# First batch of an attention, FFT and MoE kernel: the local value left in PSUM, and four unfolded feature chunks

## The chip, the cores and the metric

The kernel runs on one core of one Trainium2 chip. The metric is the device time of one execution in microseconds (us), here as the median of three. The engines are TensorE (PE, matrix products), VectorE (DVE), ScalarE (ACT), GpSimd (POOL) and SyncE (SP, which issues transfers). PE adds products in PSUM; the other data lie in SBUF.

## What is computed

The program chains three blocks, over a batch of 4 with 576 tokens, 8 heads of 64 and so 512 features:

```python
def _attn_ref(q, k, v):
    q_d, k_d, v_d = means of 4 neighbouring tokens of q, k, v
    out_up = np.repeat(sm_attn(q_d, k_d, v_d), 4, axis=2)        # coarse attention
    mask = np.abs(pos[:, None] - pos[None, :]) < 4
    out_local = softmax(where(mask, scale * q @ k.T, -1e9)) @ v  # local attention
    return out_up + out_local

def _moe_ref(x, w_ch1, w_ch2):
    u = x + np.real(np.fft.fft(np.fft.fft(x, axis=1), axis=2))
    un = (u - mean(u)) / np.sqrt(var(u) + 1e-6)
    return u + np.maximum(un @ w_ch1, 0.0) @ w_ch2               # 512 -> 2048 -> 512

def _moe2_ref(x, w_val, conv_w, w_out):
    gate = sigmoid(causal convolution of x, 5 taps for each feature)
    return (gate * (x @ w_val)) @ w_out
```

(The first lines of each are put in words.) The two blocks behind the attention work on its output with heads joined: x has 576 tokens and 512 features for each of the four batches.

## The kernel before

Features lie on the 128 partitions in four chunks of 128 (two heads each); tokens run along the free axis. The work behind the attention is cut into 12 units of 192 tokens, three for each batch. The weights come as words of 64-bit numbers: DVE unpacks them (`to_f32`, `word_op`, three steps for each block of 1024 columns, tiles `W`), they are split into a high and a low 16-bit half, and products are made as high times high, high times low and low times high. The first unit is done in 32 bits instead (`ph` L1140, `pc` L1151), because its split weights aren't ready.

The first batch is written out by hand in `chain0`. Its steps have short names, and `CHAIN0` lists them in the order in which they are recorded. `ORDER` gives, for each engine, the order of all instructions of the program; `SLOT` says which buffer of a ring each tile takes. Both are tables from a planner. So an engine does its own instructions strictly in the row given and waits on others by semaphore.

The steps of the first batch that matter here. For the local part, tokens are in three groups `GROUPS = ((0,), (1, 2), (3, 4))` of windows (232, 464 and 456 tokens), with score `S`, maximum `M`, exponential `X`, normalisation `N` (DVE, `dP`), turn `T` (PE transposes into `dPT`, ACT copies to `PT`) and value `V` (PE, into `dO`). For the coarse part there are four pairs of heads, with `s`, `m`, `x`, `n` (`E` times the reciprocal sum `lsu`, on POOL, in two halves), `t` (PE `eT`, ACT copy `ET`) and `v` (PE `po`, ACT copy to `base`, one column for four tokens).

`value` puts `dO` in two PSUM tiles, `c0` and `c1`, and ACT copies them into `X` (L1481). `base` then adds the coarse output on DVE, in place, each coarse column to its four tokens (`B` steps, four for each group, L424). The Fourier transform over features and tokens goes by symmetry. `fold` adds and subtracts chunks `c` and `c + 2` into `fs` (L1582), `fold2` adds and subtracts the two ends of the sequence into `fF` (L1589). ACT takes the high half `FH` of it (L1593), DVE the low half `FL`, and `piece` multiplies them with the features of the transform `feat` into three tiles of 96 or 97 rows (`ab`, `ab`, `eT`; L1607). There are four pieces, one for each sign `sd` and chunk `c`, of 3 tiles, 2 ends and 3 products, 72 matmuls of 127 to 129 columns.

`mirrored` (L1616, L1617) makes the mirrored chunks (`mir`) in 32 bits with two matrices, `mirror` and `corner`. From the pieces come `AH` and `AL`, sums over the sequence `pp` and `pq` (L1644), `DS`, the additions `X<-X,DS` and `X<-mir,DS`, the mean `st`, and `u` (L1690), the centred input of the first unit. A record of the profile counts a 32-bit matmul twice.

Of the kernel before, what the change touches and what calls it, by code (L numbers as in the profile page):

```python
# [1909 lines left out]
```

## Time and profile before

| | us |
|---|---|
| median of three runs (673.1 to 674.92) | 673.43 |
| the profiled execution | 673.44 |
| its span in the profile | 671.6 |
| PE busy | 649.7 (97%) |
| DVE busy | 459.2 (68%) |
| ACT busy | 321.3 (48%) |
| POOL busy | 126.6 (19%) |

The profile is of one execution. Span is the time from its first to its last recorded instruction, and an engine's busy time is a share of it. Since PE is busy for nearly all of the span, the stages in which it is not, and those in which its granted clock is low, are the ones to look at. The granted clock over the span is 0.981 of full speed in the mean.

### The profile page before, as it was taken

Reading aid. Unit: us, or ns where it says so; the run is one execution under the profiler, and the core shown is the slowest. Engines: PE = TensorE matmul, PEld = TensorE weight load, DVE = VectorE, ACT = ScalarE, POOL = GpSimd, SP = SyncE. Lnnn points to the kernel's source line nnn. Section 1 sums busy time; section 2 is a strip of 40 time slices with the busy share of each in tenths; the row PEclk is TensorE's granted clock in tenths of the full one; section 3 lists DMA queues with packets and bytes.
Section 4 is the critical chain, followed back from the end, with each engine's and each line's share of the span. In section 5 each row is a group of like instructions: output and inputs, shape, how many; then the busy total and the mean of one; then the engine's idle time right before and its main releaser. Section 6 shows DMA issues by size and latency. Waiting matters only on the chain.

```text
span 671.6 us, 18209 instructions
## 1 busy us (share of the span) xinstructions
PE 649.7 (97%) x7778; PEld 580.4 (86%) x7779; DVE 459.2 (68%) x962; ACT 321.3 (48%) x985; POOL 126.6 (19%) x178
## 2 busy tenths in 40 slices
PE   7888998999999899999999999999999999999997
PEld 3566897999998787989988889998999989999895
DVE  4989999899989877657787556676347444543354
ACT  3945546695344756775244576642232212311232
POOL 0130352023221713412010263030011010000000
PEclk9958999999999999999999999999999999999999
DMA  9992352221242012404220110000210000000001
GB/s 320 394 315 118 118 202 86 103 96 67 102 123 95 11 49 66 129 1 136 86 76 2 42 47 17 3 1 2 87 53 17 2 17 18 17 2 1 18 17 48
DMA packets 23299, 52.08 MB, mean 78 GB/s; under 512 B 1855, under 2 KB 11071, under 8 KB 22194
## 3 DMA queue, kind: packets, MB, share of 16 engines
q1 hardware_dynamic: 23218, 50.91, 22.2%
q8 instruction: 61, 1.00, 0.6%
q14 instruction: 20, 0.16, 0.1%
HBM read 44.41 MB, written 8.26 MB: 78 GB/s over the span
## 4 chain that ended last, share of the span: by engine, by line
PE 78%; DVE 10%; POOL 2%; ACT 1%; issue 0%; ACTq 0%; POOLq 0%; DVEq 0%
PE ph L1176 25%; PE pc L1196 24%; PE out L1304 7%; PE val L1288 7%; DVE W L418 3%; PE pc L1151 2%; PE ab L976 2%; PE po L908 1%; PE st L1060 1%; PE dO L785 1%; PE sc L863 1%; PE pp L999 1%; PE pq L999 1%; PE eT L898 1%; PE dPT L768 1%; POOL r L421 1%
## 5 line engine op out<-in xcount | busy, mean ns | idle before, releaser
L1176 PE MATMUL ph<-uh,W 128*128 128x192 f16 x1408 | 198.0, 246 | 0.3 <-ACT uh L1104 0.3
L1176 PEld LDWEIGHTS <-W 128*128 128x128 f16 x2112 | 176.1, 98 | 8.7 <-issue 3.8
L1176 PE MATMUL ph<-ul,W 128*128 128x192 f16 x704 | 171.5, 246 | 0.9 <-DVE ul L1105 0.9
L1196 PE MATMUL pc<-hh,W 128*128 128x192 f16 x1232 | 170.1, 246 | 0.0
L1196 PEld LDWEIGHTS <-W 128*128 128x128 f16 x1848 | 154.2, 98 | 3.9 <-issue 1.7
L1196 PE MATMUL pc<-hl,W 128*128 128x192 f16 x616 | 134.0, 246 | 0.5 <-DVE hl L418 0.5
L418 DVE SCALAR_TENSOR_TENSOR hl<-ph,hh 128x384 f16<-128x384 f32 x88 | 47.6, 550 | 89.4 <-ACT hh L1180 89.2
L1180 ACT ACTIVATE hh<-ph 128x384 f16<-128x384 f32 x88 | 42.6, 490 | 117.5 <-PE ph L1176 108.0
L418 DVE SCALAR_TENSOR_TENSOR W<-X,cw,W 128x192 f32<-128x192 f32 x160 | 63.7, 438 | 9.8 <-ACT W L1251 9.3
L1288 PE MATMUL val<-yy,W 128*128 128x192 f16 x576 | 58.9, 246 | 0.7 <-DVE yy L418 0.7
L1288 PEld LDWEIGHTS <-W 128*128 128x128 f16 x576 | 48.4, 98 | 2.1 <-issue 1.1
L1304 PE MATMUL out<-W,gh 128*128 128x512 f16 x144 | 45.9, 379 | 0.0
L749 ACT ACTIVATE dP<-dS,dmx 128x64 f32<-128x64 f32 x120 | 36.4, 334 | 1.6 <-PE dPT L768 1.4
L421 POOL TENSOR_TENSOR E<-E,lsu 72x288 f32<-72x288 f32 x16 | 18.1, 1144 | 67.2 <-DVE lsu L1515 34.0
L418 DVE SCALAR_TENSOR_TENSOR W<-W,W 128x1024 int32<-128x1024 int32 x24 | 29.5, 1240 | 0.0
L1304 PE MATMUL out<-W,gl 128*128 128x512 f16 x72 | 27.3, 379 | 1.2 <-DVE gl L418 1.2
L424 POOL TENSOR_TENSOR sq<-sq 128x384 f32<-128x384 f32 (+1 forms) x12 | 10.8, 900 | 88.8 <-ACT sq L1071 88.4
L749 ACT ACTIVATION_READ_ACCUMULATOR dP<-dS,dmx 128x1 f32 x120 | 27.1, 228 | 0.0
L1151 PE MATMUL pc<-h,W 128*128 128x192 f32 x128 | 24.2, 331 | 2.6 <-DVE W L418 2.6
L1196 PE MATMUL pc<-hh,Wz 128*128 128x192 f16 x176 | 25.6, 246 | 0.0
L1304 PEld LDWEIGHTS <-gh 128*128 128x128 f16 x144 | 14.0, 98 | 12.6 <-issue 0.2
L1140 PE MATMUL ph<-u,W 128*128 128x192 f32 x128 | 23.0, 329 | 1.0 <-DVE u L1690 1.0
(286 smaller groups left out, 1196.7 us busy)
## 6 DMA issues: line engine op xcount, KB each, us to landing
W<-in_moe_w_ch_dram SPq DMA_DIRECT2D x12, 1024.0 KB
out_dram<-osb SPq DMA_DIRECT2D x17, 256.0 KB
vw<-in_vw_dram SPq DMA_DIRECT2D x8, 512.0 KB
v<-in_vp_dram SPq DMA_DIRECT2D x24, 144.0 KB
X<-in_q_dram SPq DMA_DIRECT2D x6, 576.0 KB
kT<-in_k_dram SPq DMA_DIRECT2D x4, 582.0 KB
X<-in_moe_w_ch_dram SPq DMA_DIRECT2D x2, 1024.0 KB
raw<-in_moe_w_ch_dram SPq DMA_DIRECT2D x4, 512.0 KB
```

The costliest lines, as they stand in the source:

```text
L418: return eng.scalar_tensor_tensor(out=out, in0=in0, scalar=scalar, in1=in1, op0=op0, op1=op1)
L421: return eng.tensor_tensor(out=out, in0=a, in1=b, op=ALU.mult)
L749: A.activation(out=s_[:, z, a], in_=pss[par][:, z, a], func=AF.Exp, scale=SCALE, bias=mx[:, par, z, a:a + 1], accum_out=su[:, par, z, a:a ...
L976: T.matmul(out=ps[0:n, c0:c1], lhsT=d[x][:, c, sd, e, n0:n0 + n], rhs=feat[:, w, c, c0:c1], start=(t == 0), stop=(t == 5),)
L999: T.matmul(out=ps, lhsT=d[x][0:n, i, col:col + m], rhs=seq[0:n, j, i, w, :], start=(t == 0), stop=(t == 8),)
L1140: T.matmul(out=ps[:, e], lhsT=W[AT[kc * 2 + m // 8] + 1][:, o:o + 128], rhs=u()[:, kc, :], start=(kc == 0), stop=(kc == 3))
L1151: T.matmul(out=c["ps"][m // 2][:, m % 2], lhsT=W[9 + g][:, o:o + 128], rhs=hs[g // 2][:, g % 2, e, :], start=(kk == 0 and m % 2 == 0), sto ...
L1176: T.matmul(out=ps[:, e], lhsT=w1_ap(pw, kc, 2 * g + e), rhs=uh[px][:, kc, :], start=(t == 0), stop=(t == 11))
L1180: A.activation(out=h_, in_=ps, func=AF.Relu)
L1196: T.matmul(out=ps[m // 2][:, m % 2], lhsT=w2_ap(pw, kk, m), rhs=x[px][:, e, :], start=(kk == 0 and (pw, px) == (0, 0) and m % 2 == 0), sto ...
L1288: T.matmul(out=ps[:, e], lhsT=wv_ap(pw, kc, 2 * mh + e), rhs=m_["y"][px][:, kc, :], start=(t == 0), stop=(t == 11))
L1304: T.matmul(out=ps, lhsT=(gh, gl)[px][:, kc, t * 128:(t + 1) * 128], rhs=wo_ap(pw, kc), start=(n == 0), stop=(n == 11))
```

## The change

`value` leaves `dO` in its two PSUM tiles. `value_add` adds it to the coarse output and writes `X`, six DVE operations in all, one for each group and PSUM tile; the ACT copies and the twelve `base` additions go. `fold` takes the sum and difference of the two ends straight from `X`, for each of the four feature chunks, so `fs` and its slots go. `negated` lets ACT write part of `feat` with the opposite sign. `piece` runs over four chunks: for the first two one matmul covers both signs (255 or 257 columns); for the others there are two, of 127 to 129 columns each, the second against the negated features. That makes 36 + 72 matmuls in place of 72. `CHAIN0` takes the new steps in another order, and all tables of `ORDER` are new.

```diff
@@ SLOT @@
-    "prp.E": "01201201201201202102120120120120120120121021201201201220210210210210210210210120102102102100201201201201201201201210210210",
+    "prp.E": "0120120101202102120120120120120120121021201201201220210210210210210210210120102102102100201201201201201201201210210210",
+    "accp.acc": "0012012012012012",
...
@@ CHAIN0 @@
-m2 t0 w31 w50 x2 N2 n2 v0 w22 V0 t1 T11 w12 s3 m3 T10 v1 w32 x3 t2 w51 w70 n3 V1
-w60 v2 T21 w71 T20 t3 v3 V2 w52 w61 B00 B01 C B11 w62 E B10 B21 Z B20 A fF11 fF01 gF11
-fF00 gF01 gF00 fF10 hF11 lF11 R1 hF01 hF00 lF01 gF10 lF00 R0 hF10 eF11 lF10 eF01 w72 eF00 eF10 H0 H1 L0 L1
-H2 L2 w41 I Q0 w42 Y0 U00 U01 b0 Q1 J1 a0 o0 Y1 a2 U10 J0 U11 a1 o2 a3 b2 o1
-o3 O b1 b3
+m2 t0 w31 w50 x2 N2 n2 v0 w22 t1 w12 s3 m3 v1 w32 x3 Z t2 w51 w70 n3 w60 v2 w71
+t3 v3 V0 B00 B01 T10 T11 V1 B10 B11 T20 T21 V2 B20 B21 E A - f0 h0 f2 l0 e0 h2
+f1 l2 e2 h1 f3 l1 e1 h3 l3 R0 e3 R1 w52 w61 C w62 w72 H0 H1 L0 L1 H2 L2 w41
+I Q0 w42 Y0 U00 U01 b0 Q1 J1 a0 o0 Y1 a2 U10 J0 U11 a1 o2 a3 b2 o1 o3 O b1
+b3
...
@@ def value(g) @@
-            pos = [ps_c.tile([P, 2, nt], F32, tag=f"c{x}", name="dO") for x in range(2)]
+            pos = S_["pos", g] = [ps_c.tile([P, 2, nt], F32, tag=f"c{x}", name="dO") for x in range(2)]
...
-            xx = X.rearrange("p (a x) t -> p x a t", x=2)
-            for x in range(2):
-                A.activation(out=xx[:, x, :, PAD + q0:PAD + q0 + nt], in_=pos[x], func=AF.Copy)
+
+        def value_add(g, x):
+            q0 = 2 * GROUPS[g][0] * WQ
+            n = sum(NQ[2 * p + hf] for p in GROUPS[g] for hf in range(2)) // 4
+            o = X.rearrange("p (a x) t -> p x a t", x=2)[:, x, :, PAD + q0:PAD + q0 + 4 * n]
+            v = d["base"].rearrange("p (a x) q -> p x a q", x=2)[:, x, :, q0 // 4:q0 // 4 + n]
+            add(V, o.rearrange("p a (q r) -> p a q r", r=4), S_["pos", g][x].rearrange("p a (q r) -> p a q r", r=4),
+                v.unsqueeze(3).to_broadcast([P, 2, n, 4]))
...
-        def base(g, cs):
-            q0 = 2 * GROUPS[g][0] * WQ // 4
-            n = sum(NQ[2 * p + hf] for p in GROUPS[g] for hf in range(2)) // 4
-            for c in cs:
-                x = X[:, c, PAD + 4 * q0:PAD + 4 * (q0 + n)].rearrange("p (g r) -> p g r", r=4)
-                add(V, x, x, d["base"][:, c, q0:q0 + n].unsqueeze(2).to_broadcast([P, n, 4]))
...
-        def fold(sd, c):
-            s_ = F["s", sd, c] = prp.tile([P, S + 1], F32, tag="E", name="fs", bufs=3)
-            V.tensor_tensor(out=s_, in0=X[:, c, PAD:PAD + S + 1], in1=X[:, c + 2, PAD:PAD + S + 1],
-                            op=(ALU.add, ALU.subtract)[sd])
-
-        def fold2(sd, c):
-            s_ = F["s", sd, c]
-            F[sd, c] = mainp["tap"].tile([P, 2, HALF], F32, tag="tap", name="fF")
+        def fold(c):
+            F[c] = mainp["tap"].tile([P, 2, HALF], F32, tag="tap", name="fF")
             for e in range(2):
-                V.tensor_tensor(out=F[sd, c][:, e], in0=s_[:, 0:HALF], in1=s_[:, S:S - HALF:-1],
+                V.tensor_tensor(out=F[c][:, e], in0=X[:, c, PAD:PAD + HALF], in1=X[:, c, PAD + S:PAD + S - HALF:-1],
                                 op=(ALU.add, ALU.subtract)[e])
...
+        def negated():
+            fh["neg"] = acc_t("neg", [P, 2, 2, 256], F16)
+            for e in range(2):
+                A.activation(out=fh["neg"][:, :, :, 128 * e:128 * e + 128], in_=feat[:, :, :, FC[2 * e + 1][0]:FC[2 * e + 1][1]],
+                             func=AF.Copy, scale=-1.0)
+
+        def piece(c):
...
             for i, (n0, n) in enumerate(TT):
                 for e in range(2):
-                    c0, c1 = FC[2 * e + sd]
+                    c0, cm, c1 = FC[2 * e][0], FC[2 * e][1], FC[2 * e + 1][1]
                     for x, w in (("FH", 0), ("FH", 1), ("FL", 0)):
...
+                        ops = [(c0, c1, feat[:, w, c, c0:c1])] if c < 2 else [
+                            (c0, cm, feat[:, w, c - 2, c0:cm]), (cm, c1, fh["neg"][:, w, c - 2, 128 * e:128 * e + 128])]
+                        for k, (p0, p1, r) in enumerate(ops):
+                            T.matmul(
+                                out=fh["ab"][i][0:n, p0:p1], lhsT=d[x][:, c, e, n0:n0 + n], rhs=r,
...
```

The rows of the order below give line, operation, output, inputs and size; a line of the changed kernel is some 30 higher than the same line before. Names: `vw_156` and `vw_158` are the values of the second and third local group, `E_498` the third pair of heads, and `E_585` (before) or `E_551` (after) the fourth.

On PE, before, from the third pair's value to the mirror matmuls:

```order
L1533 MATMUL po<-ET,vr 64x144 x4
L1475 MATMUL dO<-PT,vw_156 64x58 x7
L1524 MATMUL eT<-eye,E_498 72x72 x8
L479 MATMUL tot<-ss_v_461,ones 128x1
L1475 MATMUL dO<-PT,vw_156 64x58 x25
L1533 MATMUL po<-ET,vr 64x144 x4
L1456 MATMUL dPT<-eye,dP 128x128 x8
L1475 MATMUL dO<-PT,vw_158 64x58 x24
L1475 MATMUL dO<-PT,vw_158 64x54 x8
L1524 MATMUL eT<-eye,E_585 72x72 x8
L1533 MATMUL po<-ET,vr 64x144 x4
L1616 MATMUL mir<-X,mirror 128x287
```

The same place on PE after the change:

```order
L1558 MATMUL eT<-eye,E_551 72x72 x8
L1567 MATMUL po<-ET,vr 64x144
L1485 MATMUL dPT<-eye,dP 128x128 x4
L1567 MATMUL po<-ET,vr 64x144 x3
L1504 MATMUL dO<-PT,vw_156 64x58 x2
L1485 MATMUL dPT<-eye,dP 128x128 x8
L1504 MATMUL dO<-PT,vw_156 64x58 x30
L1485 MATMUL dPT<-eye,dP 128x128 x4
L1504 MATMUL dO<-PT,vw_158 64x58 x12
L1504 MATMUL dO<-PT,vw_158 64x54 x4
L1646 MATMUL mir<-X,mirror 128x287
```

The fourth pair's turn and value moved from behind both local values to ahead of them, and the second group's turn from ahead of the third pair's value to behind the fourth's.

On DVE, before, from the last base additions to the low halves:

```order
L424 TENSOR_TENSOR X<-X,base 128x228 x2
L424 TENSOR_TENSOR X<-X,base 128x116
L424 TENSOR_TENSOR X<-X,base 128x232
L424 TENSOR_TENSOR X<-X,base 128x228 x2
L1582 TENSOR_TENSOR fs<-X 128x577 x3
L1589 TENSOR_TENSOR fF<-fs 128x289 x4
L473 TENSOR_SCALAR s_x_766<-p2b 128x1
L1589 TENSOR_TENSOR fF<-fs 128x289 x2
L1582 TENSOR_TENSOR fs<-X 128x577
L418 SCALAR_TENSOR_TENSOR FL<-fF,s_x_766,FH 128x2x289
L1589 TENSOR_TENSOR fF<-fs 128x289 x2
L418 SCALAR_TENSOR_TENSOR FL<-fF,s_x_766,FH 128x2x289 x2
```

The same place on DVE after the change:

```order
L453 TENSOR_TENSOR X<-dO,base 128x2x232 x2
L546 TENSOR_SCALAR W_117<-W_121 128x1024
L453 TENSOR_TENSOR X<-dO,base 128x2x228
L502 TENSOR_SCALAR s_x_563<-p2b 128x1
L1610 TENSOR_TENSOR fF<-X 128x289
L453 TENSOR_TENSOR X<-dO,base 128x2x228
L1610 TENSOR_TENSOR fF<-X 128x289 x3
L502 TENSOR_SCALAR iv_x_564<-p2b 128x1
L447 SCALAR_TENSOR_TENSOR FL<-fF,s_x_563,FH 128x2x289
L1610 TENSOR_TENSOR fF<-X 128x289 x4
L447 SCALAR_TENSOR_TENSOR FL<-fF,s_x_563,FH 128x2x289 x3
```

The four `fs` are gone, the additions read `dO`, and one step of unpacking stands among them.

On DVE in the later place, just ahead of the `ul` of the first unit of the second batch, before (tile names with their numbers):

```order
L796 TENSOR_REDUCE qkT_2973<-kT_2974 128x288
L418 SCALAR_TENSOR_TENSOR hl_3372<-ph_3345,hh_3370 128x384
L796 TENSOR_REDUCE qkT_2973<-X_2970 128x288
L418 SCALAR_TENSOR_TENSOR W15_121<-W17_122,s_wv_2648,W15_121 128x1024
L418 SCALAR_TENSOR_TENSOR yy_2827<-X_132,s_y0_2713,yy_2827 128x768
L418 SCALAR_TENSOR_TENSOR W15_121<-W17_122,s_wv_2648,W15_121 128x1024
L469 TENSOR_SCALAR p2a_4531<-bq1_4527 128x1
L752 TENSOR_SCALAR dsu_3039<-dsu_3039 128x8
L473 TENSOR_SCALAR iv_y0_2714<-p2b_2717 128x1
L421 TENSOR_TENSOR uc_2586<-uc_2586,r0_2600 128x768
L418 SCALAR_TENSOR_TENSOR W17_122<-W19_123,s_wo_2692,W17_122 128x1024
L1105 TENSOR_TENSOR ul_2613<-uc_2586,uh_2612 128x768
```

The same place on DVE after the change:

```order
L657 TENSOR_REDUCE cvmx_2665<-po_2656 128x1
L447 SCALAR_TENSOR_TENSOR tap_2769<-X_132,cw_108,tap_2769 128x192 x2
L447 SCALAR_TENSOR_TENSOR hl_3307<-ph_3280,hh_3305 128x384
L447 SCALAR_TENSOR_TENSOR hl_3391<-ph_3364,hh_3389 128x384
L447 SCALAR_TENSOR_TENSOR W15_121<-W17_122,s_wv_2667,W15_121 128x1024 x2
L447 SCALAR_TENSOR_TENSOR tap_2769<-X_132,cw_108,tap_2769 128x192
L447 SCALAR_TENSOR_TENSOR X_132<-pc0_2820,iv12_1525,X_132 128x2x192
L450 TENSOR_TENSOR uc_2605<-uc_2605,r0_2619 128x768
L447 SCALAR_TENSOR_TENSOR W17_122<-W19_123,s_wo_2711,W17_122 128x1024
L1134 TENSOR_TENSOR ul_2632<-uc_2605,uh_2631 128x768
```

The two reductions `qkT` and the operation on `yy` no longer stand here, and an addition to `X` does; `yy` now comes 28 rows ahead of `ul`.

## Rows read from the trace of the kernel before

**Rows 1.** Busy time by stage: start and end, length, then each engine's busy time

```profile
core 0: us, PE busy (x) PEld busy (x) DVE busy (x) ACT busy (x) POOL busy (x), PEclk, DMA share, GB/s
40.00:50.00 10.00, 9.30 (x148) 7.77 (x148) 8.60 (x18) 4.43 (x12) 2.80 (x3) 0.50 1.02 301
50.00:60.00 10.00, 8.03 (x44) 5.85 (x42) 9.28 (x22) 5.86 (x12) 0.00 (x0) 0.69 0.53 212
...
80.00:100.00 20.00, 20.00 (x215) 18.90 (x214) 19.93 (x28) 7.78 (x25) 11.76 (x14) 1.00 0.64 215
...
200.00:240.00 40.00, 36.80 (x452) 31.42 (x451) 35.99 (x62) 22.93 (x52) 16.31 (x31) 1.00 0.16 61
300.00:400.00 100.00, 99.84 (x1378) 90.84 (x1376) 69.50 (x149) 50.87 (x176) 23.01 (x31) 1.00 0.20 64
```

**Rows 2.** The same view of two single microseconds under the mirror matmuls

```profile
55.00:56.00 1.00, 1.00 (x4) 0.71 (x3) 1.00 (x4) 0.00 (x0) 0.00 (x0) 0.50 0.36 147
56.00:57.00 1.00, 1.00 (x5) 0.83 (x4) 1.00 (x5) 0.70 (x2) 0.00 (x0) 0.90 0.08 33
```

**Rows 3.** PE's waits over the span: us in total, times, longest

```profile
PE pc L1151 <- DVE W L418: 2.6, 2, 1.7
...
PE out L1304 <- DVE gl L418: 1.2, 2, 0.7
...
PE ph L1176 <- DVE ul L1105: 0.9, 1, 0.9
...
PE ab L1607 <- DVE FL L418: 0.6, 2, 0.3
```

**Rows 4.** Chain of waits of the first 125 us: start, length, what

```profile
61.49 1.12 PE ab L1607 x20
62.61 0.35 PE eT L1607 x6
...
67.43 1.14 PE pq L1644 x9
...
72.28 0.96 DVE u L1690
...
117.14 0.92 PE pc L1151 x4
```

**Rows 5.** PE's timeline: start, length, operation, records, idle time before it with its releaser

```profile
38.96 1.44 PE L1524 MATMUL eT<-eye,E 72*72 72x72 f32 x8 [1.19 <-ACT E L1509]
...
42.36 1.23 PE L1533 MATMUL po<-ET,vr 72*64 72x144 f32 x8
43.52 1.97 PE L1456 MATMUL dPT<-eye,dP 128*128 128x128 f32 x8
46.18 1.97 PE L1475 MATMUL dO<-PT,vw 64*64 64x58 f32 x64 [0.69 <-ACT PT L1459]
...
52.43 1.30 PE L1616 MATMUL mir<-X,mirror 128*128 128x287 f32 x2 [1.40 <-DVE X L424]
...
57.76 0.28 PE L1607 MATMUL ab<-feat,FH 128*96 128x128 f16 x2
```

**Rows 6.** POOL's timeline, the normalisations of the coarse part, each half one operation

```profile
20.22 2.56 POOL L421 TENSOR_TENSOR E<-E,lsu 72x288 f32<-72x288 f32 x4 [18.78 <-DVE lsu L1515]
35.77 3.75 POOL L421 TENSOR_TENSOR E<-E,lsu 72x288 f32<-72x288 f32 x2 [12.99 <-DVE lsu L1515]
41.76 2.14 POOL L421 TENSOR_TENSOR E<-E,lsu 72x288 f32<-72x288 f32 x1 [2.23 <-DVE lsu L1515]
```

**Rows 7.** DVE's timeline, first batch

```profile
51.39 1.20 DVE L424 TENSOR_TENSOR X<-X,base 128x116 f32<-128x116 f32 x4 [0.46 <-ACT base L1535]
52.51 2.09 DVE L1582 TENSOR_TENSOR fs<-X 128x577 f32<-128x577 f32 x3
54.52 1.56 DVE L1589 TENSOR_TENSOR fF<-fs 128x289 f32<-128x289 f32 x4
...
71.14 0.81 DVE L424 TENSOR_TENSOR X<-mir,DS 128x289 f32<-128x289 f32 x2
```

More of the change, by code (lines that the diff above doesn't have):

```diff
@@ L1580, in fold @@
-        def fold(sd, c):
-            s_ = F["s", sd, c] = prp.tile([P, S + 1], F32, tag="E", name="fs", bufs=3)
-            V.tensor_tensor(out=s_, in0=X[:, c, PAD:PAD + S + 1], in1=X[:, c + 2, PAD:PAD + S + 1],
-                            op=(ALU.add, ALU.subtract)[sd])
-        def fold2(sd, c):
-            s_ = F["s", sd, c]
-            F[sd, c] = mainp["tap"].tile([P, 2, HALF], F32, tag="tap", name="fF")
+            d["FH"] = mp.tile([P, 4, 2, 290], F16, tag="M", name="FH")
+            d["FL"] = mp.tile([P, 4, 2, 290], F16, tag="M", name="FL")
@@ L1595, in fold_lo, with fold_hi @@
-        def fold_lo(sd, c):
-            stt(V, d["FL"][:, c, sd, :, 0:HALF], F[sd, c], d["sx"][:, 0:1], d["FH"][:, c, sd, :, 0:HALF],
-                ALU.mult, ALU.subtract)
-        def piece(sd, c):
+        def fold_hi(c):
+            A.activation(out=d["FH"][:, c, :, 0:HALF], in_=F[c], func=AF.Copy, scale=d["sx"][:, 0:1])
+        def fold_lo(c):
+            stt(V, d["FL"][:, c, :, 0:HALF], F[c], d["sx"][:, 0:1], d["FH"][:, c, :, 0:HALF], ALU.mult, ALU.subtract)
+        def negated():
[3 more added lines that the diff above has]
+                             func=AF.Copy, scale=-1.0)
@@ L1604, in piece @@
                 for e in range(2):
-                    c0, c1 = FC[2 * e + sd]
+                    c0, cm, c1 = FC[2 * e][0], FC[2 * e][1], FC[2 * e + 1][1]
                     for x, w in (("FH", 0), ("FH", 1), ("FL", 0)):
-                        T.matmul(
-                            out=fh["ab"][i][0:n, c0:c1], lhsT=d[x][:, c, sd, e, n0:n0 + n], rhs=feat[:, w, c, c0:c1],
-                            start=(fh["e"] == 1 and (e, x, w) == (0, "FH", 0)), stop=(fh["e"] == 4 and (e, x) == (1, "FL")),
-                        )
+                        ops = [(c0, c1, feat[:, w, c, c0:c1])] if c < 2 else [
[3 more added lines that the diff above has]
+                                out=fh["ab"][i][0:n, p0:p1], lhsT=d[x][:, c, e, n0:n0 + n], rhs=r,
+                                start=(fh["e"] == 1 and (e, x, w, k) == (0, "FH", 0, 0)),
+                                stop=(fh["e"] == 4 and (e, x, k) == (1, "FL", len(ops) - 1)),
+                            )
         def mirrored(c):
@@ L1715, in chain0 @@
         for g in range(3):
-            for h in range(2):
-                tok[f"B{g}{h}"] = lambda g=g, h=h: base(g, (h, h + 2))
-        for sd in range(2):
-            for c in range(2):
-                for n, f in (("f", fold), ("g", fold2), ("h", fold_hi), ("l", fold_lo), ("e", piece)):
-                    tok[f"{n}F{sd}{c}"] = lambda sd=sd, c=c, f=f: f(sd, c)
+            for x in range(2):
+                tok[f"B{g}{x}"] = lambda g=g, x=x: value_add(g, x)
+        for c in range(4):
+            for n, f in (("f", fold), ("h", fold_hi), ("l", fold_lo), ("e", piece)):
+                tok[f"{n}{c}"] = lambda c=c, f=f: f(c)
+        tok["-"] = negated
         for c in range(2):
```

441 lines of the change are left out of this document (234 added, 207 removed), and 3 rows, old and new, of the table ORDER.

## The prediction

> **What bounds the kernel now.** I read the busy time by stage first. From 300 to 400 us PE is busy for 99.84 of 100 us at the full granted clock (1.00): there the kernel is TensorE's own work, and nothing the change touches shortens it [rows 1]. The early stages are another matter. [...] DVE works 8.60 and 9.28 us there, and 19.93 of 20 us from 80 to 100 us [rows 1]. So up to about 118 us two things race: the chain of the first batch through PE, and DVE's unpacking of the weights. PE's waits show who ends last: 2.6 us in two waits of `pc` for an unpacked `W`; at 117.14 us the chain of waits passes to PE for good [rows 3, 4]. From 200 to 240 us PE is idle for 40.00 - 36.80 = 3.2 us [rows 1], and waits for `gl` (1.2 us) and `ul` (0.9), both DVE's, are the longest of the later part [rows 3].
>
> In the first batch three places matter. The last base additions, four operations, began at 51.39 when ACT had copied `base` (0.46 us idle), took 1.20 and ended at 52.59 [rows 7]. PE waited 1.40 us for them, then did mirror and corner matmuls from 52.43 to 57.76, then the pieces [rows 5], the last of which ended at 62.61 + 0.35 = 62.96. And `u` at 72.28 starts the first unit [rows 4].
>
> **Base is finished earlier: -3.7 us.** Before, the turn and value of the last pair of heads stand behind the last local value on PE, ACT copies local values to SBUF, and DVE adds later. Now all heads go ahead of the second and third local values, and the sum is made straight from PSUM. By the order, DVE reaches the last reciprocal `lsu` with 0.8 us more work ahead of it than it had before the third one (its normalisation on POOL began at 35.77 [rows 6]), so at about 36.4. POOL normalised four halves in 2.56 us, 0.64 each, and later two in 3.75 [rows 6]; two halves so cost 1.3 to 3.75 us, and I take 2.5, the middle, since both conditions of DVE occur here: 38.9. Then the second half of `eT` (1.44 for both), its copy by ACT, the second half of `po` (1.23 for both) and the copy to `base` [rows 5], together 2.4 with the two copies at about 0.5: 41.3. Ends are 40.1 and 43.
>
> From there: the first additions 0.3 (later ones run beside PE), the eight `dPT` (1.97 in all, of which 0.5 is done by then) 1.5, the second local value like the third one now, 1.97 for 64 records and 1.85 without its last ones, four `dPT` 1.0, a copy of `PT` by ACT 0.6, and the second half of the third local value 0.95 [rows 5]: 41.3 + 0.3 + 1.5 + 1.85 + 1.0 + 0.6 + 0.95 = 47.5. The last two additions cost about 0.55 us each (456 elements; two of 289 took 0.81) with a fold of 0.39 between and the rest of the queue, 1.4 in all: 48.9 against 52.59, so -3.7 [rows 7]. Ends: -1.5 with the late base, -4.5 if PE waits for no copy.
>
> The six additions now read `dO` in PSUM, which no addition in this trace does. The nearest rows: `X<-mir,DS` (PSUM) took 0.405 us each, `fF` (both inputs in SBUF, as wide) 0.39 [rows 7]; I price the two alike. [...]
>
> **Mirror to pieces: +1.4 us.** Six of the eight mirror and corner operations (12 of the 14 records in 57.76 - 52.43 = 5.33 us [rows 5]) stand ahead of the first piece now: 4.6 us. They start on the first chunks at 48.0, so the pieces begin at 52.6 and not at 57.76. Four such records ran in 1.00 us at a clock of 0.50 and five at 0.90 [rows 2]; all at the lower level they would end at 54. Then the pieces. Before, 72 matmuls of 127 to 129 columns took 1.12/20 = 0.056 us each [rows 4], 4.0 in all, and 5.2 with their waits (57.76 to 62.96). After, there are 36 of 255 or 257 columns and 72 of 127 to 129. The wide ones lie between 0.056 and the 1.14/9 = 0.127 us of 289 columns [rows 4]; by columns, 0.113. So 36 x 0.113 + 72 x 0.056 = 8.1 us, and 52.6 + 8.1 = 60.7 against 62.96: -2.3. Since the last chunk's 27 matmuls are written tile by tile, its first two tiles close earlier than before, worth 0.2. So `u` falls from 72.28 to 69.8, **-2.5 us**.
>
> **DVE's own work: neutral by 118 us.** Four `fs` go (2.09/3 = 0.70 us each, 2.8 in all); the eight `fF` (0.39) stay and read `X`; twelve additions become six over the same width [rows 7]. ACT loses six copies and gains two sign changes; it was busy for only 5.86 of 10 us from 50 to 60 [rows 1], and the sign changes stand beside PE's mirror matmuls. Without that cover they would cost about 1 us. PE waited 0.6 us for two `FL` among the pieces [rows 3]; with the mirror matmuls ahead and twice the columns that goes. The order puts 1.3 us more unpacking before `u`, so DVE leads by 3.8 us there; but 1.5 us of conversion was moved ahead of the second unit's `ul`, so DVE's lead at 100 to 118 us is 2.3, no more than PE's 2.5, and PE's 2.6 us of waits [rows 3] stay. I count nothing, with -1.3 and +0.2 as ends.
>
> **200 to 240 us: -0.5.** Ahead of the `ul` there, the order leaves DVE two reductions `qkT` and one `yy` fewer. But PE's idle time there is 3.2 us in all [rows 1] and other waits follow behind `ul`, so I take 0.5; ends 0 and -2. POOL's queue keeps its work. On SP's one load of w1 stands later, and the features come earlier; no wait of these rows is one for a DMA.
>
> **The sum.** -2.5 + 0 - 0.5 = -3.0 us. The profiled execution took 673.44 us with a span of 671.6, so 1.84 us lie outside it; the median of the runs is 673.43, the same. The span becomes 668.6 and the time 670.4.
>
> **The rivals.** *DVE is the bound all the way to 118 us* (faster, 668.1 to 669.6). For it: 19.93 of 20 us busy from 80 to 100 [rows 1]. Then what leaves DVE counts whole: 2.8 for `fs` and 0.46 of idle time [rows 7], and 0.5 to 2 from the later stage, -3.8 to -5.3. Against it: PE is busy for 20.00 us in the same stage [rows 1].
>
> *The normalisation on POOL is held up* (no change, 671.9 to 673.9). One half of head pair 3 took 2.14 us and two halves of pair 2 took 3.75, where others took 0.64 each, while DVE was unpacking [rows 6]. If both halves take 2.14 us, 4.3 in all, and pair 2's delays them too, `base` comes 1.8 to 3 us later than I put it and the gain is 0 to 1.5. [...]
>
> *The pieces run at the lower clock* (slower, 674.5 to 679). The granted clock rose to 0.90 in the 57th us, when PE had worked on mirror matmuls without a gap from 52.43 on [rows 2, 5]; before that PE had waited 1.40. Now the pieces follow six such operations, with shorter waits ahead, and there are 8.1 us of them. [...] It decides once more than about 4.5 us of piece time stands at the lower level, which costs as much again: 3.0 eats the gain and 1.5 to 2.0 passes the bound. Against it: four mirror records at the lower level and five near the full one [rows 2] show the rise 3.6 us after the gap, before the pieces.
>
> *The new order opens waits of PE between 118 and 240 us* (674 to 677): the 1.5 us of conversion ahead of `ul` turn into a wait, and so do other steps moved there. That *the change does nothing*, because the six copies were hidden, lies inside the POOL case: 673.4.
>
> **How the numbers follow.** Forecast, 669.6 to 671.9: 0.44. DVE-bound: 0.13. POOL: 0.22. Lower clock: 0.09. New waits: 0.12. The bound of 0.3% is 2.0 us, 671.4 to 675.5, about what a measurement of this kernel can tell from no change. Of the forecast 0.35 lies below it, with DVE-bound's 0.13: faster 0.48. Slower: 0.09 and half of the new waits: 0.15. The rest is 0.37. The range leaves out the lower clock and most of the new waits, and reaches 0.5 below the DVE case: 667.6 to 674.8.
>
> **What would show it.** In the profile after: the last addition from PSUM ends near 48.9; the mirror matmuls start near 48.0 and the first piece near 52.6; the last piece ends near 60.7, `u` starts near 69.8, the granted clock is 1.00 under the pieces, PE's waits for `W` before 118 us keep 2.6 us, and idle time from 200 to 240 is below 3.2. It is wrong if the last piece ends after 62.96, if a half of pair 3's normalisation takes 2 us, or if `u` is 2.5 us ahead and the end is not.

## The result: 665.24 us, and the gain is not where it was forecast

The changed kernel took 665.24 us in the median (664.39 to 666.91) against 673.26 for the kernel before in the same measurement: a ratio of 0.988 (95% interval 0.987 to 0.989), 8.0 us less, where 3.0 were forecast. Timed again on two other occasions the ratio was 0.991 (0.989 to 0.993) and 0.990 (0.988 to 0.991), that is 5.6 and 6.8 us less. The profiled execution took 665.45 us with a span of 663.7, so it can be set beside that of before (673.44 and 671.6).

The busy time by stage, after (columns as in [rows 1]):

```profile
30.00:40.00 10.00, 10.00 (x70) 6.81 (x69) 8.12 (x20) 7.49 (x41) 3.42 (x5) 0.52 1.05 335
40.00:50.00 10.00, 9.83 (x148) 7.69 (x148) 7.48 (x17) 4.40 (x10) 0.00 (x0) 0.62 1.01 311
50.00:60.00 10.00, 9.87 (x105) 8.73 (x102) 9.61 (x19) 6.97 (x13) 0.00 (x0) 1.00 0.76 293
80.00:100.00 20.00, 20.00 (x196) 19.06 (x195) 19.30 (x27) 9.70 (x36) 6.09 (x6) 1.00 0.60 208
100.00:120.00 20.00, 18.87 (x294) 17.47 (x291) 19.91 (x23) 12.61 (x49) 9.17 (x13) 1.00 0.37 124
200.00:240.00 40.00, 39.86 (x506) 35.77 (x504) 34.45 (x68) 24.94 (x72) 16.45 (x25) 1.00 0.18 65
300.00:400.00 100.00, 100.00 (x1373) 91.24 (x1371) 66.94 (x137) 50.23 (x169) 24.75 (x35) 1.00 0.21 70
```

Before, the stage from 100 to 120 us read:

```profile
100.00:120.00 20.00, 17.43 (x230) 16.06 (x229) 19.93 (x25) 10.96 (x41) 5.37 (x7) 1.00 0.22 79
```

From 200 to 240 us PE's idle time fell from 3.2 us [rows 1] to 0.14. From 50 to 60 PE is busy for 9.87 us at the full granted clock, where before it was 8.03 at 0.69 [rows 1]. PE's waits after:

```profile
PE ph L1205 <- DVE ul L1134: 1.0, 1, 1.0
PE sc L1527 <- DVE tr L450: 0.7, 1, 0.7
...
PE st L1084 <- DVE u L1720: 0.5, 1, 0.5
```

Of the waits of [rows 3], those of `pc` for `W`, `out` for `gl` and `ab` for `FL` are gone; a wait for `ul` of 1.0 us, now at 114 us, is the longest one left in the work behind the start.

Now the same view with the span cut in two at the start of `u`. First the kernel before, then the changed one:

```profile
0.00:72.28 72.28, 61.47 (x676) 41.83 (x676) 59.38 (x117) 43.87 (x175) 11.72 (x24) 0.83 0.76 267
72.28:671.60 599.32, 588.20 (x7102) 538.53 (x7103) 399.86 (x846) 277.44 (x811) 114.87 (x155) 1.00 0.17 55
```

```profile
0.00:72.40 72.40, 68.39 (x728) 46.62 (x731) 57.36 (x111) 45.00 (x176) 9.56 (x27) 0.88 0.79 275
72.40:663.70 591.30, 585.81 (x7093) 538.07 (x7093) 399.70 (x842) 274.26 (x806) 109.99 (x151) 1.00 0.16 54
```

This is the result in four lines. `u` has not moved (72.28, 72.40). Ahead of it PE's idle time fell by 6.8 us (72.28 - 61.47 = 10.81, now 4.01), and 6.9 us more busy time fills it. Behind `u` the time is 8.0 us shorter: 5.6 us less idle time (11.12, now 5.49) and 2.4 us less busy time. The trace places those 5.6 us: 1.4 at 100 to 120 us, 3.1 at 200 to 240, 0.6 just behind `u`, 0.5 at 180 to 200.

More busy time is not the same as more work. Count each record of PE up to the start of the next one. Then the pieces take 3.5 us more ahead of `u`, the steps moved there from behind it 1.4, and the mirror and corner matmuls 1.4 less. Another 3.7 us lie in the 535 records ahead of the mirror matmuls, which are as many as before but took 46.6 us in place of 42.9. Why is not shown: some 150 of them ran at the lower clock of 0.50 (30.5 to 47.5 us), before some 195 (32.4 to 52.4), but they stand in smaller rows. Eight scores `sc` in one row took 1.2 us before, and in rows of 2, 2 and 4 they took 2.5 after, both at a granted clock of 0.50. Behind `u`, too, only some 0.7 of the 2.4 us are steps that went ahead; the rest is spread over operations that are as many as before (`dO` 0.5 us less, `out` 0.4, `val` 0.35).

The start itself, on PE after the change (columns as in [rows 5]; the rows are from two stretches):

```profile
50.47 2.58 PE L1646 MATMUL mir<-X,mirror 128*128 128x287 f32 x8
...
53.86 0.38 PE L1636 MATMUL ab<-feat,FH 128*96 128x257 f16 x2
...
61.80 0.22 PE L1636 MATMUL eT<-neg,FL 128*96 128x128 f16 x1
61.86 1.19 PE L1647 MATMUL mir<-X,corner 128*128 128x289 f32 x4
...
72.29 0.65 PE L764 MATMUL dS<-X 64*58 64x64 f32 x26
...
73.41 0.59 PE L1084 MATMUL st<-X,ones 128*128 128x192 f32 x2 [0.46 <-DVE u L1720]
```

On POOL (columns as in [rows 6]), and on DVE (as in [rows 7]):

```profile
32.49 2.09 POOL L450 TENSOR_TENSOR E<-E,lsu 72x288 f32<-72x288 f32 x2 [9.50 <-DVE lsu L1549]
38.19 0.66 POOL L450 TENSOR_TENSOR E<-E,lsu 72x288 f32<-72x288 f32 x1 [3.60 <-ACT ET L1561]
...
38.84 0.66 POOL L450 TENSOR_TENSOR E<-E,lsu 72x288 f32<-72x288 f32 x1
```

```profile
43.95 0.40 DVE L453 TENSOR_TENSOR X<-dO,base 128x232 f32<-128x232 f32 x1 [1.15 <-ACT base L1569]
...
51.07 0.63 DVE L453 TENSOR_TENSOR X<-dO,base 128x456 f32<-128x456 f32 x1
...
72.40 0.95 DVE L1720 TENSOR_TENSOR u<-X,st 128x768 f32<-128x768 f32 x1 [0.57 <-PE st L1716]
```

### The profile page after: what moved, and what is told of

The parts are those of the page before. It is cut to its first block, busy times and chain, and to the rows that moved or that the text cites. A ratio compares the mean times of both kernels' runs of the same rounds, so it can differ in the third digit from the quotient of the medians.

```text
span 663.7 us, 18283 instructions
## 1 busy us (share of the span) xinstructions
PE 654.2 (99%) x7815; PEld 584.7 (88%) x7815; DVE 457.1 (69%) x952; ACT 319.3 (48%) x981; POOL 119.5 (18%) x178
## 4 chain that ended last, share of the span: by engine, by line
PE 91%; DVE 5%; ACT 1%; DMA 1%; issue 1%; SPq 0%; ACTq 0%
PE ph L1205 26%; PE pc L1225 26%; PE val L1317 7%; PE out L1333 7%; DVE W L447 2%; PE pc L1180 2%; PE ab L1005 2%; PE ph L1169 2%; PE dO L814 1%; PE po L937 1%; PE sc L892 1%; PE st L1089 1%; PE pq L1028 1%; PE pp L1028 1%; PE dS L764 1%; PE eT L927 1%
## 5 line engine op out<-in xcount | busy, mean ns | idle before, releaser
L1205 PE MATMUL ph<-uh,W 128*128 128x192 f16 x1408 | 202.4, 246 | 0.2 <-ACT uh L1133 0.2
L1225 PE MATMUL pc<-hl,W 128*128 128x192 f16 x616 | 129.1, 246 | 0.0
L447 DVE SCALAR_TENSOR_TENSOR W<-X,cw,W 128x192 f32<-128x192 f32 x160 | 67.2, 454 | 1.4 <-ACT W L1280 1.2
L450 POOL TENSOR_TENSOR E<-E,lsu 72x288 f32<-72x288 f32 x16 | 14.3, 909 | 63.3 <-DVE lsu L910 26.5
L1351 ACT ACTIVATE osb<-out,sof 128x512 f32<-128x512 f32 x15 | 10.3, 687 | 27.8 <-PE out L1333 27.8
L1225 PEld LDWEIGHTS <-Wz 128*128 128x128 f16 x264 | 22.2, 98 | 0.8
```

Source lines behind the costliest of these rows:

```text
L447: return eng.scalar_tensor_tensor(out=out, in0=in0, scalar=scalar, in1=in1, op0=op0, op1=op1)
L450: return eng.tensor_tensor(out=out, in0=a, in1=b, op=ALU.mult)
L1205: T.matmul(out=ps[:, e], lhsT=w1_ap(pw, kc, 2 * g + e), rhs=uh[px][:, kc, :], start=(t == 0), stop=(t == 11))
L1225: T.matmul(out=ps[m // 2][:, m % 2], lhsT=w2_ap(pw, kk, m), rhs=x[px][:, e, :], start=(kk == 0 and (pw, px) == (0, 0) and m % 2 == 0), sto ...
```

## The experiments

Every ratio below is to the kernel before, timed on the same chip. h1 to h7 shared one chip; c1, h8 and h9, and on a later occasion c2, h9b, h3b and h4b, were timed on another. "Rest" is the span less the time at which `u` starts on DVE, both from the one profiled execution.

| kernel | ratio (95%) | `u` | span | rest |
|---|---|---|---|---|
| before | 1 | 72.28 | 671.6 | 599.3 |
| changed | 0.988 (0.987 to 0.989) | 72.40 | 663.7 | 591.3 |
| h1: old start, new rest | 0.997 (0.996 to 0.998) | 72.06 | 669.6 | 597.5 |
| h2: new start, old rest | 1.013 (1.012 to 1.015) | 72.62 | 681.2 | 608.6 |
| h5: h1 with the total of w1 later | 0.994 (0.992 to 0.996) | 72.64 | 668.5 | 595.9 |
| h3: new additions, old transform | 0.992 (0.991 to 0.993) | 74.25 | 666.1 | 591.9 |
| h4: old additions, new transform | 0.993 (0.991 to 0.995) | 74.00 | 666.1 | 592.1 |
| h6: 36 narrow matmuls left out | 0.987 (0.985 to 0.990) | 70.29 | 661.5 | 591.2 |
| h7: h3 with two `fs` on POOL | 0.995 (0.993 to 0.997) | 75.50 | 667.4 | 591.9 |
| c1: changed, again | 0.991 (0.989 to 0.993) | 72.10 | 664.2 | 592.1 |
| h8: old additions and transform, new order | 0.997 (0.996 to 0.998) | 77.58 | 670.6 | 593.0 |
| h9: moved work back behind `ph` | 0.992 (0.990 to 0.993) | 73.17 | 668.5 | 595.3 |
| c2: changed, again | 0.990 (0.988 to 0.991) | 73.98 | 665.2 | 591.2 |
| h9b | 0.996 (0.994 to 0.998) | 71.75 | 666.2 | 594.5 |
| h3b | 0.997 (0.995 to 0.998) | 76.10 | 668.0 | 591.9 |
| h4b | 0.993 (0.992 to 0.995) | 75.48 | 668.3 | 592.8 |

The last column is the finding. Where the new order of the rest follows the new start and no step is moved back (as in h9 and h9b), the rest is 591.2 to 593.0 us, whether `u` starts at 70.3 or at 77.6. So in the profiled executions each microsecond by which `u` is earlier or later goes through to the end, and the 8 us of the changed kernel lie behind `u`: they have to do with the order of the rest, which needs the new start, and not with an earlier `u`. The column `u` itself differs by up to 1.9 us between executions of one kernel (72.10, 72.40 and 73.98 for the changed one), so it is compared below between profiles in which POOL took the same 2.09 us for two normalisations.

### The start and the rest apart (h1, h2, h5)

h1 has the code of before and its order up to `u`, and behind `u` the order of the changed kernel; h2 is the other half. h5 is h1 with the total of w1 and the scores of the second batch moved on PE behind the first eight `ph` (and ACT's steps likewise). The edits, in words for h1 and h2 and in PE's rows for h5:

```diff
 h1: ORDER of the kernel before
-rows behind u: as before
+rows behind u: as in the changed kernel
 h2: ORDER of the changed kernel
-rows behind u: as in the changed kernel
+rows behind u: as before
 h5: h1, on PE
+L1160 MATMUL ph<-u_1005,W_114 128x192 x2
+L1160 MATMUL ph<-u_1005,W_115 128x192 x2
...
 L499 MATMUL tot<-ss_w_1058,ones 128x8
 L745 LDWEIGHTS bandb
```

> The code and the order of the kernel before up to the operation u of the first unit, then what is left in the order of the kernel after. In the traces u starts at 72.28 us before and at 72.40 after, and PE is idle for 7.4 us behind it before and 1.7 after. Theory A (the gain comes from the order behind u alone): most of the 5.7 us of idle time goes, 666.5 to 669. Theory B (what is done ahead of u, in code and order, lets the rest run without waits): no gain here, 671 to 674.

> The changed code and its order up to u, then what is left in the order of the kernel before. Theory A: the waits behind u stay, and only the 2.1 us of PE work that the new start does ahead of u is won, 670 to 672. Theory B: 665 to 667.5. If both halves are needed together, this run and the one with the old start are both slower than the sum of their parts says, by over 2 us.

> The old start with the new rest, as in the first of these runs, but PE's first eight products of the first unit (ph) stand ahead of the sum total of the squares of w1, on which PE had waited for 2.3 us there, and the steps on ACT behind it follow. Theory A (the order of the rest is worth most of the idle time whatever the start): 666.5 to 669, that is 3 us or more below the run before it. Theory B (the new rest needs what the new start has done by u): 670 to 672.

h1 came out at 672.05 us, in the range of its second theory, h2 at 683.02, above both of its ranges, and h5 at 670.06, at the lower edge of its second one. The busy time from 100 to 120 and from 200 to 240 us, of h1 and of h2:

```profile
100.00:120.00 20.00, 18.84 (x219) 17.39 (x217) 19.93 (x22) 9.65 (x35) 12.90 (x14) 1.00 0.52 175
200.00:240.00 40.00, 39.80 (x505) 35.31 (x504) 34.65 (x69) 24.10 (x60) 15.42 (x30) 1.00 0.21 74
```

```profile
100.00:120.00 20.00, 11.56 (x64) 10.66 (x63) 19.97 (x26) 7.95 (x37) 9.08 (x13) 0.75 0.43 146
200.00:240.00 40.00, 38.02 (x513) 34.56 (x512) 33.26 (x62) 23.52 (x54) 10.40 (x26) 1.00 0.20 65
```

h1 has the code and the start of before and yet only 1.16 and 0.20 us of idle time there, where the kernel before had 2.57 and 3.20: the order behind `u` closes both stages by itself. It opens one wait, however, because the old start finishes the squares of w1 (`Wz`) late; the new rest wants their total at once. PE's waits in h1, h5 and h2:

```profile
PE tot L499 <- ACT Wz L590: 2.3, 1, 2.3
```

```profile
PE ph L1196 <- DVE hl L438: 1.5, 1, 1.5
...
PE dS L745 <- ACT p2t L502: 1.3, 1, 1.3
```

```profile
PE pc L1158 <- DVE W L425: 6.5, 1, 6.5
```

With the total moved later (h5) the rest is 595.9, so the order behind `u` is worth 3.4 us on the old start (by the ratio of h5, 4.1), and two waits stand in the place of the one. The other half is no half at all: the new start with the old rest is 9 us slower than before, mostly in one wait of 6.5 us for an unpacked `W`, presumably since the old rest takes the unpacking in a row that the new start no longer prepares. The two tables are made for each other, and what one half is worth depends on the other.

### The two edits of the code (h3, h4, h8, h3b, h4b)

h3 keeps the additions from PSUM and puts back `fs`, `fold2` and the 72 matmuls; h4 does the reverse; h8 puts both back. All three have the new order, with the old steps where the new ones stood.

```diff
 h3: fold, piece
-V.tensor_tensor(out=F[c][:, e], in0=X[:, c, PAD:PAD + HALF], ...)
+s_ = F["s", sd, c] = prp.tile([P, S + 1], F32, tag="E", name="fs", bufs=3)
+V.tensor_tensor(out=s_, in0=X[:, c, PAD:PAD + S + 1], in1=X[:, c + 2, ...], op=(ALU.add, ALU.subtract)[sd])
+V.tensor_tensor(out=F[sd, c][:, e], in0=s_[:, 0:HALF], ...)
 h4: value, value_add
-pos = S_["pos", g] = [...]
+A.activation(out=xx[:, x, :, PAD + q0:PAD + q0 + nt], in_=pos[x], func=AF.Copy)
...
+add(V, x, x, d["base"][:, c, q0:q0 + n].unsqueeze(2).to_broadcast([P, n, 4]))
```

> The changed kernel with its order, but the transform of the kernel before in it: four folds fs of 577 elements on DVE (0.70 us each), 72 pieces of 127 to 129 columns, no negated features. PE does about 4.0 us less (36 x 0.111), DVE 2.8 us more. If the pieces stand on the path to the end, since PE has no idle time left: 661 to 663.5. If DVE's chain of folds sets the start of the pieces and its work the rest: 664.5 to 668.

> The changed kernel with its order, but the local value copied out of PSUM by ACT and the coarse output added in place by twelve DVE operations, as before. If the addition from PSUM is what brings base forward: a copy of 0.5 us twice and its semaphores stand between the last value and the last addition, 666 to 668. If it is hidden by the mirror matmuls and ACT's room: 664.7 to 666.

> The old addition and the old transform together, in the new order of the start and of the rest. If the two parts of the code add up (2.6 and 3.3 us in the runs that undo one): 5 to 7 us above the changed kernel, 670 to 672, with u near 76. If they cover for each other, because PE waits for one while the other runs: 2.5 to 4.5 us above it. The new order alone would then be worth 1.5 to 3 or 4 to 5.5 of the 8 us.

> The changed kernel once more, on the chip on which the next three are timed, as their yardstick. Two earlier measurements gave ratios of 0.9883 and 0.9908 to the kernel before; I expect 0.986 to 0.992 (664.5 to 668.5 us), u of the profile at 72 to 73 and 591 to 592.5 us behind it.

> Additions from PSUM with the old folded transform in the new order, beside the changed kernel on one chip. If each microsecond of u goes through to the end: 1.5 to 2.5 us above the changed kernel of this call. Rival, that a later u is absorbed behind it: within 0.8 us.

> ACT copies and twelve additions with the new transform in the new order, beside the changed kernel on one chip. If each microsecond of u goes through to the end: 1.3 to 2.3 us above the changed kernel of this call. Rival, that a later u is absorbed behind it: within 0.8 us.

In the new order the old transform costs 1.85 us at `u` (74.25 against 72.40), the old additions 1.6, and both together 5.2. So the new start order by itself would have made `u` 5.3 us later than before (77.58), and the code pays that back. Beside the changed kernel on one chip the timed medians are 4.8 us (h3b), 2.2 us (h4b) and 3.6 us (h8) higher, the spans of the profiled executions 2.8, 3.1 and 6.4 us. h4b lies in its first range, h3b above both of its ranges, as h3 and h4 did (668.61 and 668.81 us); h8's 3.6 us lie in its second range and its 671.75 us in its first. So the sign of each cost is shown, but its size in the time is not: at `u` the two costs are more than additive, in the medians less.

How the old transform loses: busy time of h3 from 50 to 70 us, then of h3b.

```profile
50.00:60.00 10.00, 6.56 (x64) 5.09 (x61) 9.49 (x19) 4.47 (x7) 0.00 (x0) 1.00 0.68 262
60.00:70.00 10.00, 7.85 (x68) 5.14 (x66) 9.97 (x18) 6.77 (x16) 0.40 (x6) 1.00 0.01 2
```

```profile
50.00:60.00 10.00, 7.52 (x68) 5.91 (x63) 9.48 (x20) 4.44 (x8) 0.00 (x0) 0.88 0.75 292
60.00:70.00 10.00, 8.38 (x64) 5.52 (x63) 9.39 (x15) 6.39 (x16) 0.40 (x6) 0.84 0.01 2
```

DVE is the engine that is busy (9.97 of 10 us in h3), and PE waits among the pieces, 2.6 us in all for `FL` in h3, where the new transform leaves it 0.13 us idle from 50 to 60. In h3b the granted clock was 0.88 and 0.84 as well, and there `u` is another 1.85 us later; h3, with more idle time, kept 1.00, so what makes it fall is not shown. With the new transform and the new additions it was 1.00 from 50 to 70 us in each of the seven profiles. So leaving out the four `fs` on DVE, 2.8 us by [rows 7], is worth 1.85 to 3.7 us at `u`, although PE does twice the columns.

h8 shows why the two costs are more than additive at `u`: its additions end later, and its mirror matmuls run at a lower granted clock (0.64 in the mean from 50 to 60 us, after 1.00; 4.15 us for the eight records that took 2.58 after):

```profile
53.16 4.15 PE L1639 MATMUL mir<-X,mirror 128*128 128x287 f32 x8
```

### Work moved ahead of u's wait (h9, h9b)

In the changed kernel the first scores of the second batch and the total of w1 stand among the last steps ahead of `u`. h9 puts them behind the first eight `ph` on PE, with ACT's steps likewise; all else stays.

```diff
-L508 MATMUL tot<-ss_w_1077,ones 128x8
...
-L754 MATMUL dS<-bandb 128x256
...
-L764 MATMUL dS<-X 58x64 x13
...
 L1169 MATMUL ph<-u_1024,W_115 128x192 x2
+L508 MATMUL tot<-ss_w_1077,ones 128x8
+L754 LDWEIGHTS bandb
+L754 MATMUL dS<-bandb 128x256
+L764 MATMUL dS<-X 58x64 x2
```

> The changed kernel once more, on the chip of the two runs beside it: 0.987 to 0.990 of the kernel before, as measured first.

> The changed kernel, with the first scores of the second batch (dS, 16 products and two with the band) and the sum total of the squares of w1 on PE behind the first eight products ph of the first unit, where the kernel before had them, and the two steps of ACT behind the total moved likewise. If it is this work that fills PE's waits for X and u: PE idle 1.5 to 2.2 us longer between 69 and 75 us, and the end 1.5 to 2.5 us later. If other work takes its place or what follows catches up: under 0.7 us.

> Scores of the second batch and the total of w1 behind the first eight ph again, beside the changed kernel on one chip. If the work that stands ahead of u's wait is part of the gain: 1.5 to 2.5 us above the changed kernel of this call, with 2 us more idle time of PE from 70 to 80 us and u where it was. Rival, that this work only fills time which is given back later: within 1 us of the changed kernel. If the first profile's held normalisation on POOL (4.12 us for two halves) was chance, it is about 2.1 us here.

The first timing gave no difference from the changed kernel beside it (0.992 and 0.991), as the rival has it, the second 3.9 us more (670.73 against 666.84), above the other range, with runs from 667.49 to 674.57. The profiles agree with each other: the rest is 595.3 and 594.5, that is 2.4 to 4.1 us longer than in the three profiles of the changed kernel. The stretch behind `u` in h9b and in c2:

```profile
70.00:80.00 10.00, 7.71 (x71) 6.69 (x71) 9.17 (x15) 0.65 (x3) 3.20 (x3) 1.00 0.26 72
```

```profile
70.00:80.00 10.00, 9.54 (x84) 8.21 (x82) 9.36 (x18) 3.93 (x9) 2.30 (x6) 1.00 0.16 54
```

PE idles 2.29 us there instead of 0.46. Between executions in which POOL took the same time the span is 2.0 to 2.5 us longer (h9b against the changed kernel and c1) and 3.3 us longer (h9 against c2). So this work did fill a wait that the start has anyway, and it is part of the gain; its size in the timed medians lies between nothing and 4 us, and these runs don't settle it.

### The price of the pieces, and DVE's help (h6, h7)

h6 leaves out 36 of the narrow matmuls, so that part of the transform is missing. h7 is h3 with two of the four `fs` on POOL and the pieces in an order to suit.

```diff
 h6: piece
-(c0, cm, feat[:, w, c - 2, c0:cm]), (cm, c1, fh["neg"][:, w, c - 2, 128 * e:128 * e + 128])]
+(c0, cm, feat[:, w, c - 2, c0:cm])]
 h7: fold of h3
-V.tensor_tensor(out=s_, ...)
+(G if sd else V).tensor_tensor(out=s_, ...)
```

> The changed kernel without the 36 matmuls of the pieces that multiply with the negated features (so a part of the transform is left out): 36 x 0.057 = 2.05 us less work for PE ahead of u, nothing less for DVE. If PE's work ahead of u is what counts there, u starts 2.0 us earlier and the end comes 1.8 to 2.6 us earlier: 662.5 to 664 by the ratio. If DVE's unpacking is the bound behind u, u is earlier and the end less than 0.7 us.

> The new addition and order with the old transform, but the two folds with the minus sign (fs, 577 elements) on GpSimd, which has nothing to do there, and the plus pieces first. DVE has 1.4 us less and PE's waits of 2.6 us for the low halves FL should shrink. If DVE's chain is what costs the old transform its gain: u near 72.0 in place of 74.25 and 663.5 to 666. If POOL and DVE hold each other up (both read two inputs from SBUF): FL no earlier, 667 to 670.

Without 36 matmuls, 36 x 0.056 = 2.0 us of PE, `u` came 2.1 us earlier and the span was 2.2 us shorter: PE bounds this stretch now, and the pieces cost what they take. The timed median of h6 (665.31 us, above its range; 0.987, 0.985 to 0.990) cannot tell 2 us from the changed kernel on another chip. h7's `fs` on POOL:

```profile
51.40 2.00 POOL L1603 TENSOR_TENSOR fs<-X 128x577 f32<-128x577 f32 x1 [12.26 <-issue]
54.23 1.79 POOL L1603 TENSOR_TENSOR fs<-X 128x577 f32<-128x577 f32 x1 [0.83 <-DVE fF L1610]
```

One takes 1.79 to 2.00 us there against 0.70 on DVE [rows 7], the pieces wait 2.2 us for one `FL`, and `u` is 1.25 us later than in h3, at a granted clock of 0.92 and 0.91 from 50 to 70 us where h3 had 1.00. The time, 670.60 us, is that of the second theory. No kernel here that does all the work beats the changed one.

## Why the prediction was wrong, step by step

The total was wrong because the terms behind `u` were sized at nothing and at 0.5 us; the terms ahead of `u` were wrong as well, the other way.

**Base earlier (forecast -3.7, measured -0.9).** The last addition ends at 51.70 (51.07 + 0.63), not at 48.9, and the mirror matmuls start at 50.47, not at 48.0. The step that failed is base ready at 41.3, with 43 as its late end: the addition that waits for it starts at 43.95. I had chained its waits, `lsu`, POOL, `eT`, copy, `po`, as if PE were free for each. `lsu` is ready at 38.0, not at 36.4, since DVE waited 1.4 us for PE's scores; POOL took 1.3 us for the two halves, not 2.5, which was luck, and was done at 39.50 (forecast 38.9). From there to `base` it took 4.4 us and not 2.4. After the change PE is busy for 10.00 of 10.00 us from 30 to 40, at a granted clock of 0.52, and the turns and values stand in one queue with the local values. What I took for a chain of latencies was a queue of work. The clock was not the error, since I had priced each step from rows at the lower level, 0.50 (the eight `dPT` took 1.97 us again). PE's clock rises to the higher level, 1.00, in the 48th us, where before it rose in the 57th [rows 2]:

```profile
46.00:47.00 1.00, 1.00 (x41) 1.00 (x45) 0.62 (x1) 0.00 (x0) 0.00 (x0) 0.50 1.02 408
47.00:48.00 1.00, 1.00 (x33) 0.94 (x28) 0.30 (x1) 0.10 (x1) 0.00 (x0) 0.74 1.04 407
48.00:49.00 1.00, 0.83 (x18) 0.59 (x18) 1.00 (x3) 1.00 (x3) 0.00 (x0) 1.00 1.06 420
```

**The additions from PSUM (forecast alike, right; their width, wrong).** In the same order 232 elements took 0.39 and 0.40 us from PSUM (after) and 0.39 from SBUF (h8). So pricing the two alike by the nearest rows was right: the runs show a difference of at most 0.01 us. But the wide ones take 0.63 to 0.64, not 0.55: two in-place additions of 228 took 0.70 together, so the fused one saves about 0.07 us.

**Mirror to pieces (forecast -2.3 for the last piece, measured -0.9).** Six mirror and corner operations took 3.4 us, not 4.6, because they ran at the higher clock (1.00 from 50 to 60 us); that brought half of the late start back, and the first piece stood at 53.86 (forecast 52.6). The pieces end at 62.02, 8.2 us later (forecast 8.1, right). What I left out of the path are the last two corner operations, which now run behind the last piece, 1.19 us at 61.86; before, one of them stood ahead of the pieces and one among the means, at 69.67. With them, and the steps that were moved in among the means, `u` came at 72.40 and not at 69.8: 1.3 us from the late start, the rest from what stands behind the pieces. Two readings were wrong without moving the sum. The four records in 1.00 us of [rows 2] are those that touch that microsecond; at the lower clock of 0.50 one took 0.48 us (two, from 54.48 to 55.44, took 0.96), and that is what gives the 54. And the last chunk has 36 matmuls, not 27.

**100 to 118 us (forecast 0 with -1.3 and +0.2 as ends, measured -1.4).** I weighed DVE's lead, 2.3 us, against PE's 2.5 us of waits, and let the waits stay. But PE's order changed as well: the `ph` of the first unit now follow `u` in one row of 64 records (10.4 us), and its `pc`, which need the unpacking, stand later (by 93 us 22 records of them had run before, 2 after). So PE works where DVE used to be late, and DVE meets PE once, at `ul`, for 1.0 us. DVE's lead at `u` had no part in it: h1, with the old start, has 1.16 us of idle time there, the changed kernel 1.13. I had compared one engine's queue with the old waits of the other.

**200 to 240 us (forecast -0.5 with -2 as an end, measured -3.1).** The argument was that `ul` stands behind fewer operations, but that other waits follow behind it. The waits shrank together. DVE before, then after:

```profile
228.57 0.95 DVE L1105 TENSOR_TENSOR ul<-uc,uh 128x768 f16<-128x768 f32 x1
...
233.07 1.15 DVE L418 SCALAR_TENSOR_TENSOR gl<-tap,gh 128x384 f16<-128x384 f32 x1
...
235.04 1.34 DVE L418 SCALAR_TENSOR_TENSOR gl<-tap,gh 128x384 f16<-128x384 f32 x1
```

```profile
222.99 0.95 DVE L1134 TENSOR_TENSOR ul<-uc,uh 128x768 f16<-128x768 f32 x1
...
226.57 0.56 DVE L447 SCALAR_TENSOR_TENSOR gl<-tap,gh 128x384 f16<-128x384 f32 x1
...
227.84 0.56 DVE L447 SCALAR_TENSOR_TENSOR gl<-tap,gh 128x384 f16<-128x384 f32 x1
```

`ul` came 5.6 us earlier, the two `gl` 6.5 and 7.2 us. The kernel as a whole was some 4.9 us ahead there (8.0 less this stage's 3.1), so each of these gained on PE, and each more than the one ahead of it. That is not for fewer operations between `ul` and the second `gl` (nine before, ten after), but because the same operations took less time. A `gl` took 1.15 and 1.34 us before and 0.56 after. For an operation on a single column DVE has, before and after:

```profile
234.14 0.65 DVE L421 TENSOR_TENSOR ivvo<-iv_wv,iv_wo 128x1 f32<-128x1 f32 x1
```

```profile
224.85 0.15 DVE L450 TENSOR_TENSOR ivvo<-iv_wv,iv_wo 128x1 f32<-128x1 f32 x1
```

Before, POOL did three additions beside them, from 232.02 to 235.96; after, it did nothing from 224.5 to 230.4. PE's wait for `gl` goes with the order behind `u`: none of the fourteen profiles with the new one lists it, and in h2, with the old one, it is 1.2 us in two waits, as before. That POOL's additions are what holds DVE up is read from their overlap; no run moved them alone. I had read DVE's queue ahead of one wait, kept the waits behind it as they were, and counted no change on POOL.

**What the sum did not have.** 2.4 us less of PE's busy time stands behind `u`, in part (some 0.7 us) because steps were moved ahead of it into time that PE waited, and 1.1 us of idle time went in two places that I had not looked at (just behind `u`, and 180 to 200 us). I had asked what each edit does to the moment of `u`. An order can fill the wait instead and leave `u` where it is.

**The rivals.** *DVE is the bound to 118 us* named the right stretch, but DVE's 19.93 us of 20 [rows 1] only fell to 19.30 from 80 to 100 us, and the gain there came from the order behind `u` (h1). *The lower clock under the pieces* did not come: 1.00 from 50 to 60 us. It did come in h3b, under the old transform, at a granted clock of 0.88 and 0.84: three matmuls of the pieces took 0.17 us there at 55.5 us, 0.32 between 57.6 and 60.8, and 0.17 again from 61.2 on. That is nearly the as much again that I had counted for the lower level; no run shows all the pieces at it, so the upper end of 679 was an estimate. *New waits from 118 to 240 us* did not come: 0.14 us idle from 200 to 240. *The normalisation on POOL is held up* is real, but not in the profile above (2.09 us for the two halves). It is in c2, on POOL and on DVE:

```profile
32.50 4.13 POOL L450 TENSOR_TENSOR E<-E,lsu 72x288 f32<-72x288 f32 x2 [9.52 <-DVE lsu L1549]
```

```profile
73.98 0.95 DVE L1720 TENSOR_TENSOR u<-X,st 128x768 f32<-128x768 f32 x1 [0.57 <-PE st L1716]
```

These are the halves of pair 2; those of pair 3 took 0.66 us each in every profile of the new start. Two more microseconds on POOL, and `u` 1.6 to 1.9 us later than in the other two profiles of this kernel. h9 against h9b and h4b against h4 show the same, with 4.1 us against 2.1 and `u` 1.4 to 1.5 us later. I had put `base` 1.8 to 3 us later by it; the addition that waits for `base` starts at 45.16 in c2, 1.2 us later than in the profile above, so the price was somewhat high. Even so c2 with it is 1% faster than the kernel before, since the gain lies behind `u`.

My chances leaned on `u`. The prediction would have counted `u` ahead and the end not as proof of an error; what came is the reverse, the end ahead and `u` not, and none of its three signs of an error appeared.

## What to carry to other kernels

Cut the span at the event that you expect to move, and account for busy and idle time on both sides of it: an earlier event, a filled wait and a better order behind it are three different gains. Where a planner has laid all queues anew, a stage with idle time is not worth the first wait in it alone; follow every wait of the stage through the new queues of both engines. A chain of latencies was too short here on a full engine, 2.4 us forecast and 4.4 measured with PE busy for 10.00 of 10 us; there count the work that is queued ahead of each link, at the clock that it has (0.52). And look at what runs beside an operation as well as ahead of it: the DVE operation `gl` took 0.56 us with POOL at rest, and 1.15 and 1.34 with POOL at work beside it.
